# A mixture-of-experts kernel on one core: the place of one row copy in ScalarE's order

## The chip, the cores and the metric

The kernel runs on 1 core of one Trainium2 chip. The metric is the device time of one execution in microseconds (us); lower is better. All times below are in us unless ns stands beside them. The engines are called as in the profile: PE (TensorE), PEld (TensorE's weight loads, which overlap PE), DVE (VectorE), ACT (ScalarE), POOL (GpSimd), SP (SyncE, which here issues DMAs).

## What is computed

A causal convolution over the sequence, with one 7-tap softmax filter for each of 8 heads, gives 28672 rows of 192 numbers. Each row with a positive skip score is then sent to the one of 8 experts whose gate logit is largest, and the expert's two-layer network, scaled by the softmax of that logit, is added to the row:

```python
out = np.einsum('hk,bskhg->bshg', softmax(weight), windows(x))     # (8, 3584, 192)
x = out.reshape(28672, 192)
do_compute = x @ w_skip > 0
xc = x[do_compute]
logits = xc @ w_gate                                               # 8 experts
e_idx = np.argmax(logits, axis=1)
gate_w = softmax(logits)[np.arange(len(xc)), e_idx]
for e in range(8):
    mask = e_idx == e
    h = np.maximum(xc[mask] @ w1[e], 0.0)                          # 192 -> 1024
    y[mask] = gate_w[mask, None] * (h @ w2[e])                     # 1024 -> 192
x[do_compute] = xc + y
```

## The kernel before, in words

The first part (to about 175 us) computes the convolution and the router batch by batch and writes the convolved rows to `out` in device memory. It then makes, for each expert, a list of its rows. The second part goes over these lists in blocks of 256 rows (a few of 128), 61 blocks in all, numbered n: 0 to 7 are from experts 0 and 1 and run while the router finishes; from n = 8 (`NTAIL`) on come 3 more blocks for each of experts 0 and 1 (8 to 13), then 6 for each of experts 2 to 7 (14 to 49; expert e begins at block 14 + 6(e − 2)), then 11 blocks (50 to 60) whose expert is looked up at run time, with weights `wd` that are loaded back from a scratch tensor `wscr`.

All matrix products run in float16, and each number is carried as a high and a low part. For one block there are four steps:

- `gather` (L827): POOL fetches the block's rows by indirect DMA into `y`.
- `prep` (L842): DVE finds a power-of-two scale for each row, ACT writes the scaled high part `yt` (L854), DVE the low part (L859), and SP issues one DMA transpose per 128 rows (L862), which puts the block's columns into `m`, with four slots of 256 rows. Slot 0 holds the high part of the 128 first columns, slot 1 the 64 last columns, high part in partitions 0 to 63 and low part in 64 to 127, slot 2 the low part of the 128 first.
- `up` (L875), the first layer: PE makes 1024 hidden numbers in four PSUM banks `ph`. ACT evicts each bank with a ReLU into `hh` (L908), DVE writes the low part `hl` (L910).
- `down` (L913), the second layer: 24 matmuls of three kinds (L938 to L940) for each 128 rows into `po`; DVE adds the rows (L920), POOL scatters them back (L922).

The step that the change touches lies between `prep` and `up`. The low part of the weights for the 64 last columns is a product with only 64 rows of the array in use. In a block of 256 rows from n = 8 on (`paired`), two such products are put side by side, one in the lower and one in the upper half of the array (L893 to L896). The upper one needs the 64 rows of slot 1 in partitions 64 to 127, so ACT copies them there, into slot 3 (`upper_half`, L838 to L840):

```python
nc.scalar.copy(k.m[64:P, 3, :], k.m[0:64, 1, :])
...
for f, p0, m in ((a + j, 0, 1), (a + fs + j, 64, 3)):
    o = OW1L + F + f * P
    nc.tensor.matmul(phs[f - j][:, j, :], wt[p0:p0 + 64, o:o + P], k.m[p0:p0 + 64, m, 0:w], ...)
```

The copy needs both transposes of its block. Of the eight matmuls (L895) with which such a block opens, the first needs only slot 1, the second needs the copy.

The order on each engine is the order in which the code is written (a manual schedule). The main loop (L1162) writes for each n: the copy of block n+1, `up` of block n+1, `down` of block n. So PE runs up(n+1), down(n), up(n+2), down(n+1) and so on. `weave` (L1143) puts other work between the pieces: after each piece of `up` (four) and `down` (two) `tail_slot` takes one step of background work, then some steps of `prep` follow, which is begun for block n+3 while up(n+1) is written.

The background work is above all `split_weights` (L265), which turns the next expert's float32 weights into high and low parts: seven ACT conversions of 128x512 (L303), each followed a step later by its low part on DVE (L314) and two stores to `wscr` on SP (L318). The first of the seven waits for the scale `ar` (L338, DVE). With six blocks to an expert, the first conversion stands in the second piece of the down in front of the expert's last block; the next three follow the last block's first three evictions of `ph`, and the last three stand between its fourth eviction and the first eviction of the next expert's first block.

Of the kernel before, what the change touches and what calls it, by code (L numbers as in the profile page):

```python
# [16 lines left out]
P = 128  # L17
# [75 lines left out]
def conv_router_moe(ctx: ExitStack, tc: tile.TileContext, x, weight, w_skip, w_gate, w1, w2, out):  # L93
    nc = tc.nc
# [231 lines left out]
    def new_wt(e):  # L326
        if e % 3 == 2:
            return wk3.tile([P, WW], F16, tag="wt", bufs=1, name=f"wt{e}")
        return wst.tile([P, WW], F16, tag="wt", bufs=2, name=f"wt{e}")
# [68 lines left out]
    def store_y(b, half, c0=0, c1=NC):  # L398

        first, n = HALVES[half]  # L400
        t = ys[b, half]
        c0, c1 = max(c0, first), min(c1, first + n)
        full = min(c1, NC - 1)
        for t0, t1 in zip(RSPLIT, RSPLIT[1:]):
            nc.sync.dma_start(out=out[b * S + R * c0:b * S + R * full, :].rearrange("(c t) d -> t c d", t=R)[t0:t1],
                              in_=t[t0:t1, c0 - first:full - first])
        if c1 == NC:
            nc.sync.dma_start(out=out[b * S + R * (NC - 1):(b + 1) * S, :], in_=t[0:LAST, n - 1])
# [426 lines left out]
    def paired(k):  # L835
        return k.us == 2 and NTAIL <= k.n < NBLK

    def upper_half(k):  # L838
        if paired(k):
            nc.scalar.copy(k.m[64:P, 3, :], k.m[0:64, 1, :])  # L840

    def prep(k):  # L842

        am = k.am = wk2.tile([P, 2], F32, tag="yam", bufs=6, name=f"yam{k.n}")
        sc = wk2.tile([P, 2], F32, tag="ysc", bufs=3, name=f"ysc{k.n}")
        nc.vector.tensor_reduce(out=am[:, 0:k.us], in_=k.y[:, 0:k.us], axis=AX.X, op=ALU.max, apply_absolute_value=True)
        yield
        for t, s, op in ((am, am, ALU.bitwise_and), (sc, am, ALU.bitwise_xor)):
            nc.vector.tensor_scalar(out=t[:, 0:k.us].bitcast(I32), in0=s[:, 0:k.us].bitcast(I32), scalar1=EXPMASK,  # L849
                                    scalar2=None, op0=op)  # L850
            yield
        yt = wk2.tile([P, 2, 2 * D], F16, tag="yt", bufs=3, name=f"yt{k.n}")
        for u in range(k.us):
            nc.scalar.activation(yt[:, u, 0:D], k.y[:, u, 0:D], AF.Copy, scale=sc[:, u:u + 1])  # L854
        yield
        k.m = wk2.tile([P, 4, BLK], F16, tag="m", bufs=MBUF, name=f"m{k.n}")
        for u in range(k.us):
            for (a, b_, o) in ((P, D, D), (0, P, D + 64)):
                nc.vector.scalar_tensor_tensor(out=yt[:, u, o:o + b_ - a], in0=k.y[:, u, a:b_],  # L859
                                               scalar=sc[:, u:u + 1], in1=yt[:, u, a:b_],  # L860
                                               op0=ALU.mult, op1=ALU.subtract)
            nc.sync.dma_start_transpose(out=k.m[:, 0:3, u * P:(u + 1) * P], in_=yt[:, u, :])  # L862
            yield

    def finish(gen):
# [5 lines left out]
    def bank(pools):  # L871
        pools.append(pools.pop(0))
        return pools[-1]

    def up(k, wt):  # L875
        k.hh = wk3.tile([P, NF, BLK], F16, tag="hh", bufs=2, name=f"hh{k.n}")
        k.hl = wk3.tile([P, NF, BLK], F16, tag="hl", bufs=2, name=f"hl{k.n}")
        w = k.us * P
        fs = 2 * BLK // w
        seq = ((OW1, 0), (OW1, 2), (OW1 + F, 1), (OW1L, 0), (OW1L + F, 1))  # L880
        phs = {}

        def open_bank(f0):
            phs[f0] = bank(ph_pools).tile([P, 2 * BLK], F32, tag="ph", name=f"ph{k.n}_{f0}").rearrange(
                "p (f w) -> p f w", w=w)

        if paired(k):

            for f0 in range(0, NF, fs):
                open_bank(f0)  # L890
            for a in range(0, NF, 2 * fs):
                for j in range(fs):
                    for f, p0, m in ((a + j, 0, 1), (a + fs + j, 64, 3)):  # L893
                        o = OW1L + F + f * P
                        nc.tensor.matmul(phs[f - j][:, j, :], wt[p0:p0 + 64, o:o + P], k.m[p0:p0 + 64, m, 0:w],  # L895
                                         start=(j == 0), stop=False, tile_position=(p0, 0), skip_group_check=True)  # L896
            seq = seq[:-1]
        for f0 in range(0, NF, fs):
            if not paired(k):
                open_bank(f0)  # L900
            ph = phs[f0]
            for f in range(f0, f0 + fs):
                for n, (o, m) in enumerate(seq):
                    nc.tensor.matmul(ph[:, f - f0, :], wt[:, o + f * P:o + (f + 1) * P], k.m[:, m, 0:w],  # L904
                                     start=(n == 0 and not paired(k)), stop=(n == len(seq) - 1),
                                     skip_group_check=paired(k))
            hh = k.hh[:, f0:f0 + fs, 0:w]
            nc.scalar.activation(hh, ph, AF.Relu)  # L908
            yield
            nc.vector.scalar_tensor_tensor(out=k.hl[:, f0:f0 + fs, 0:w], in0=ph, scalar=0.0, in1=hh,  # L910
                                           op0=ALU.max, op1=ALU.subtract)
# [36 lines left out]
    blocks = []  # L948
# [22 lines left out]
    NBLK = len(blocks)  # L971
# [15 lines left out]
    def weights_of(n):  # L987
        k = blocks[n]
        return wts[k.e] if k.l is None else dynw[k.l]
# [141 lines left out]
    def tail_slot():  # L1131

        background()
        if not listed:
            turns((routes, 0), (routes, 1), (inversions, 0))
            if not routes and not inversions:
                finish(final_lists())
                listed.append(True)
        elif tables:
            if next(tables[0], tables) is tables:  # L1140
                tables.pop()

    def weave(gen, preps=(), n=0):  # L1143

        for _ in gen:
            tail_slot()
            for _ in range(n):
                for p in list(preps):
                    if next(p, p) is p:
                        preps.remove(p)  # L1150
                    else:
                        break
# [9 lines left out]
    for n in range(NBLK):  # L1162
        k = blocks[n]
        if 0 < n < 5:
            store_y(B - 1, n // 3, 8 * n - 8, min(8 * n, NC))
        if n == NTAIL:
            while not past:
                next(tables[0])
            ph1.close()
            wk4 = ctx.enter_context(tc.tile_pool(name="wk4", bufs=1))  # L1170
            ph_pools.append(ctx.enter_context(tc.tile_pool(name="ps_h2", bufs=2, space=PSUM)))
            ph_pools.append(ps_h)
            po_pools.append(ctx.enter_context(tc.tile_pool(name="ps_o2", bufs=2, space=PSUM)))
        nxt = 2 if n == NTAIL - 2 else k.e + 1 if k.e is not None and k.e >= NA and n == first_of[k.e] else E
        if nxt < E:
            wts[nxt] = new_wt(nxt)
            bg.append(split_weights(nxt, wts[nxt]))
        if n + 1 < NBLK and n + 1 == first_of.get(blocks[n + 1].e) and (blocks[n + 1].e or 0) >= NA:
            background(-1)
        m = n + PREP + 1  # L1180
        if m < NBLK and blocks[m].l is not None:
            l = blocks[m].l
            dynw[l] = wk4.tile([P, WW], F16, tag="wd", bufs=5, name=f"wd{l}")
            bg.append(dyn_weights(l, dynw[l]))
        while prepped < min(n + PREP + 1, gathered):
            ahead.append(prep(blocks[prepped]))
            prepped += 1
        if n + 1 < NBLK:
            upper_half(blocks[n + 1])
            weave(up(blocks[n + 1], weights_of(n + 1)), ahead, PU)  # L1190
        ready = NBLK if listed and n > 3 else NTAIL
        if n + 1 >= NTAIL - 2:
            while prepped < min(n + 3, gathered):
                ahead.append(prep(blocks[prepped]))
                prepped += 1
        while gathered < min(n + AHEAD + 1, ready):
            gather(blocks[gathered])
            gathered += 1
        weave(down(k, weights_of(n)), ahead, PD)
        if n + 2 < NBLK and not hasattr(blocks[n + 2], "m"):  # L1200
            if prepped < n + 3:
                ahead.append(prep(blocks[prepped]))
                prepped += 1
            finish(ahead.pop(0))
        if n >= NTAIL + 8 and n % 2 == 0 and (n - NTAIL - 8) // 2 < NDYN:
            dyn_lists((n - NTAIL - 8) // 2)
# [4 lines left out]
    with tc.If(left > 0):  # L1211
# [13 lines left out]
        for e in range(E):  # L1225
            first = nc.values_load(lo_hi[0:1, e:e + 1], min_val=0, max_val=NTOK // BLK)
            last = nc.values_load(lo_hi[0:1, E + e:E + e + 1], min_val=0, max_val=NTOK // BLK)
            with tc.For_i(first, last, 1) as i:
                k = Blk()
# [37 lines left out]
```

## Time and profile before

| what | value |
|---|---|
| time, median of 3 runs | 700.04 (698.31 to 700.28) |
| the profiled execution | 694.53 |
| span in its profile, first to last instruction | 692.8 |
| granted TensorE clock, mean | 0.993 |
| busy: PE, DVE, ACT, POOL | 661.6, 516.5, 338.8, 269.9 |
| start of the first and of the last copy (L840), 48 in all | 259.6, 657.4 |

Rows of the timeline and of the groups read: start and length in us, engine, line of the kernel, operation, output <- input, tile, count, and in brackets how long the engine had stood idle before and what ended that. In the list of waits, a row gives the waiting engine and line, what it waited for, then us in all, times, and the longest. Where the brackets are missing, the engine had no idle time to speak of. Consecutive rows may overlap, since an engine takes the next instruction before the one in front has ended.

### The profile page before, as it was taken

The numbers are of one execution on the slowest core, as the hardware profiler recorded it, in microseconds if no ns is written. First come the engines' busy times: TensorE is split into PE (matmuls) and PEld (weight loads), VectorE is DVE, ScalarE is ACT, GpSimd is POOL, SyncE is SP. The second block draws the span as 40 slices with busy tenths as digits, with TensorE's granted clock in tenths as the row PEclk, the third lists the DMA queues.
The fourth block names the chain that finished last, engine by engine and source line by source line (L and its number), as shares of the span: only waits on it lengthen the run. The fifth ranks groups of instructions, "written<-read, shape, count | busy, mean of one in ns | idle before, by whom it ended". The sixth has DMA issues, their size and how long they took to land. (4 is left out here: it accounts for less than half of the span.)

```text
span 692.8 us, 17693 instructions
## 1 busy us (share of the span) xinstructions
PE 661.6 (96%) x6597; PEld 562.8 (81%) x6597; DVE 516.5 (75%) x1462; ACT 338.8 (49%) x695; POOL 269.9 (39%) x299
## 2 busy tenths in 40 slices
PE   8999899999899999799999999999999999999995
PEld 7667666765689888699888888888888889988995
DVE  7068689878999979678778778778778776666652
ACT  5775486547732333454454554553543644434421
POOL 3111102127013354554644543544444455454322
PEclk9999999999999999999999999999999999999999
DMA  7999999934833455464357365563564446999970
GB/s 211 344 332 323 311 305 330 337 105 99 269 101 95 127 135 112 115 179 133 99 174 155 107 184 130 131 189 105 126 186 118 120 131 162 279 304 286 311 202 15
DMA packets 154403, 129.51 MB, mean 187 GB/s; under 512 B 59600, under 2 KB 141266, under 8 KB 154308
## 3 DMA queue, kind: packets, MB, share of 16 engines
q1 hardware_dynamic: 143268, 106.49, 53.8%
q0 software_dynamic: 11040, 21.80, 12.0%
q8 instruction: 54, 0.88, 0.5%
q14 instruction: 41, 0.34, 0.2%
HBM read 69.70 MB, written 48.04 MB: 170 GB/s over the span
## 5 line engine op out<-in xcount | busy, mean ns | idle before, releaser
L908 ACT ACTIVATE hh<-ph 128x512 f16<-128x512 f32 x230 | 134.5, 594 | 237.6 <-PE ph L904 177.0
L910 DVE SCALAR_TENSOR_TENSOR hl<-ph,hh 128x512 f16<-128x512 f32 x230 | 156.9, 686 | 83.2 <-ACT hh L908 46.1
L940 PE MATMUL po<-wt,hl 128*128 128x192 f16 x768 | 188.9, 246 | 0.9 <-issue 0.9
L938 PE MATMUL po<-wt,hh 128*128 128x192 f16 x768 | 188.9, 246 | 0.9 <-issue 0.7
L939 PE MATMUL po<-wt,hh 128*128 128x192 f16 x768 | 188.9, 246 | 0.5 <-issue 0.4
L904 PE MATMUL ph<-m,wt 128*128 128x256 f16 (+1 forms) x1680 | 186.4, 268 | 2.7 <-DVE yam L849 0.9
L904 PEld LDWEIGHTS <-wt 128*128 128x128 f16 x1680 | 154.2, 98 | 28.8 <-issue 12.4
L922 POOL DMA_INDIRECT out_dram<-o,rows x82 | 84.8, 1035 | 150.5 <-DVE o L920 122.4
L830 POOL DMA_INDIRECT y<-out_dram,rows x82 | 86.1, 1049 | 27.9 <-issue 22.6
L938 PEld LDWEIGHTS <-hh 128*128 128x128 f16 x920 | 90.0, 98 | 2.8 <-issue 2.2
L939 PEld LDWEIGHTS <-hh 128*128 128x128 f16 x920 | 90.0, 98 | 1.8 <-issue 1.2
L940 PEld LDWEIGHTS <-hl 128*128 128x128 f16 x920 | 90.0, 98 | 1.5 <-issue 1.3
L361 PE MATMUL pc<-xs,toep 128*120 128x384 f32 (+1 forms) x224 | 79.8, 480 | 0.0
L920 DVE SCALAR_TENSOR_TENSOR o<-po,yf,y 128x192 f32<-128x192 f32 x115 | 46.6, 414 | 31.4 <-PE po L940 17.2
L363 ACT COPY ys<-pc 120x768 f32<-120x768 f32 (+1 forms) x56 | 42.7, 763 | 43.1 <-PE pc L361 33.4
L859 DVE SCALAR_TENSOR_TENSOR yt<-y,ysc,yt 128x64 f16<-128x64 f32 x230 | 57.8, 311 | 2.6 <-ACT yt L854 2.6
L854 ACT ACTIVATE yt<-y,ysc 128x192 f16<-128x192 f32 x115 | 46.2, 448 | 26.9 <-DVE ysc L849 20.0
L361 PEld LDWEIGHTS pc<-xs,toep 128*120 128x120 f32 x224 | 37.6, 187 | 14.6 <-issue 1.7
L282 DVE TENSOR_REDUCE am<-raw 128x1 f32<-128x512 f32 x56 | 37.9, 676 | 7.8 <-DMA raw<-in_moe_w_dram 7.5
L314 DVE SCALAR_TENSOR_TENSOR wt<-raw,ar,wt 128x512 f16<-128x512 f32 x56 | 41.3, 744 | 1.9 <-ACT wt L303 1.9
L303 ACT ACTIVATE wt<-raw,ar 128x512 f16<-128x512 f32 x56 | 38.8, 727 | 5.1 <-DVE ar L338 5.1
L922 POOL DMA_INDIRECT out_dram<-o,rowsa x14 | 15.5, 1108 | 58.1 <-DVE o L920 49.2
(203 smaller groups left out, 897.8 us busy)
## 6 DMA issues: line engine op xcount, KB each, us to landing
wd<-wscr SPq DMA_DIRECT2D x44, 449.0 KB
wscr<-wt SPq DMA_DIRECT2D x84, 128.0 KB
xs<-in_x_dram SPq DMA_DIRECT2D x7, 1440.0 KB
xs<-in_x_dram SPq DMA_DIRECT2D x7, 1248.0 KB
out_dram<-ys SPq DMA_DIRECT2D x6, 1344.0 KB
out_dram<-ys SPq DMA_DIRECT2D x6, 1092.0 KB
raw<-in_moe_w_dram SPq DMA_DIRECT2D x32, 192.0 KB
raw<-in_moe_w_dram SPq DMA_DIRECT2D x8, 512.0 KB
```

What stands on the lines that cost most here:

```text
L361: nc.tensor.matmul(pc[0:R, i, 0:n * G], toep[:, h + i, :], xs[b, half][:, :, (h + i) * G:(h + i + 1) * G], start=True, stop=True)
L830: rows_apart(nc.gpsimd.indirect_dma_start(out=k.y[:, u, 0:D], out_offset=None, in_=out[0:k.rows, :], in_offset=bass.IndirectOffsetOnAxis(a ...
L854: nc.scalar.activation(yt[:, u, 0:D], k.y[:, u, 0:D], AF.Copy, scale=sc[:, u:u + 1])
L859: nc.vector.scalar_tensor_tensor(out=yt[:, u, o:o + b_ - a], in0=k.y[:, u, a:b_], scalar=sc[:, u:u + 1], in1=yt[:, u, a:b_], op0=ALU.mult, ...
L904: nc.tensor.matmul(ph[:, f - f0, :], wt[:, o + f * P:o + (f + 1) * P], k.m[:, m, 0:w], start=(n == 0 and not paired(k)), stop=(n == len(se ...
L908: nc.scalar.activation(hh, ph, AF.Relu)
L910: nc.vector.scalar_tensor_tensor(out=k.hl[:, f0:f0 + fs, 0:w], in0=ph, scalar=0.0, in1=hh, op0=ALU.max, op1=ALU.subtract)
L920: nc.vector.scalar_tensor_tensor(out=o[:, u, :], in0=po, scalar=f2[:, u:u + 1], in1=k.y[:, u, 0:D], op0=ALU.mult, op1=ALU.add)
L922: rows_apart(nc.gpsimd.indirect_dma_start(out=out[0:k.rows, :], out_offset=bass.IndirectOffsetOnAxis(ap=k.si[:, u, 0:1], axis=0), in_=o[:, ...
L938: nc.tensor.matmul(pos[u], hh, w2(OW2, f), start=(f == 0), stop=False)
L939: nc.tensor.matmul(pos[u], hh, w2(OW2L, f), start=False, stop=False)
L940: nc.tensor.matmul(pos[u], hl, w2(OW2, f), start=False, stop=(f == NF - 1))
```

## The change

`upper_half` is given a block's number instead of the block, remembers which copies are written (`raised`), and asks whether the block's transposes are written already (`turned`, filled by `prep`). The main loop calls it twice: for block n+1 ahead of up(n+1), as before, and for block n+2 directly behind up(n+1), so ahead of down(n). The first call writes nothing if the copy is written already.

```diff
-    def upper_half(k):
-        if paired(k):
-            nc.scalar.copy(k.m[64:P, 3, :], k.m[0:64, 1, :])
+    turned, raised = set(), set()
+
+    def upper_half(n):
+        if n < NBLK and paired(blocks[n]) and n in turned and n not in raised:
+            raised.add(n)
+            nc.scalar.copy(blocks[n].m[64:P, 3, :], blocks[n].m[0:64, 1, :])
...
             nc.sync.dma_start_transpose(out=k.m[:, 0:3, u * P:(u + 1) * P], in_=yt[:, u, :])
+            if u == k.us - 1:
+                turned.add(k.n)
             yield
...
         if n + 1 < NBLK:
-            upper_half(blocks[n + 1])
+            upper_half(n + 1)
             weave(up(blocks[n + 1], weights_of(n + 1)), ahead, PU)
+            upper_half(n + 2)
```

Only ACT's order is changed by it, and there at eleven places. (A name's first number is the block or the expert: `m19` belongs to block 19, `wt3` to expert 3. Line numbers are 3 to 5 higher with the change: L843 is the copy, L913 the eviction.) The first place is block 19, the last block of expert 2, with the last evictions of block 18 ahead of it, on ACT before:

```order
L908 ACTIVATE hh18_5118<-ph18_4_5122 128x512
L908 ACTIVATE hh18_5118<-ph18_6_5123 128x512
L303 ACTIVATE wt3_4675<-raw3_4700,ar3_5019 128x512
L840 COPY m19_5021<-m19_5021 64x256
L908 ACTIVATE hh19_5263<-ph19_0_5265 128x512
```

And the same place on ACT with the change:

```order
L913 ACTIVATE hh18_5118<-ph18_4_5122 128x512
L913 ACTIVATE hh18_5118<-ph18_6_5123 128x512
L843 COPY m19_5021<-m19_5021 64x256
L303 ACTIVATE wt3_4676<-raw3_4700,ar3_5019 128x512
L913 ACTIVATE hh19_5263<-ph19_0_5265 128x512
```

The copy of block 19 has moved ahead of the first conversion of expert 3's weights, the one that waits for the scale. The second place is block 20, the first block of expert 3, on ACT before:

```order
L908 ACTIVATE hh19_5263<-ph19_6_5268 128x512
L303 ACTIVATE wt3_4675<-raw3_4700,ar3_5019 128x512 x3
L840 COPY m20_5172<-m20_5172 64x256
L908 ACTIVATE hh20_5439<-ph20_0_5441 128x512
L908 ACTIVATE hh20_5439<-ph20_2_5442 128x512
```

And the same place on ACT with the change:

```order
L913 ACTIVATE hh19_5263<-ph19_6_5268 128x512
L303 ACTIVATE wt3_4676<-raw3_4700,ar3_5019 128x512
L843 COPY m20_5172<-m20_5172 64x256
L303 ACTIVATE wt3_4676<-raw3_4700,ar3_5019 128x512 x2
L913 ACTIVATE hh20_5439<-ph20_0_5441 128x512
```

The copy of block 20 has moved ahead of the last two of the three conversions; the one that is left ahead of it is written by the background step behind the last piece of `up`. The same two moves stand at the blocks 25 and 26, 31 and 32, 37 and 38, 43 and 44.

The eleventh place is block 13, where expert 2's weights are converted, on ACT before:

```order
L908 ACTIVATE hh12_4262<-ph12_6_4267 128x512
L303 ACTIVATE wt2_3594<-raw2_3619,ar2_4037 128x512 x2
L840 COPY m13_4220<-m13_4220 64x256
L908 ACTIVATE hh13_4386<-ph13_0_4388 128x512
L303 ACTIVATE wt2_3594<-raw2_3619,ar2_4037 128x512
```

And with the change, on ACT at block 13:

```order
L913 ACTIVATE hh12_4262<-ph12_6_4267 128x512
L303 ACTIVATE wt2_3594<-raw2_3619,ar2_4037 128x512
L843 COPY m13_4221<-m13_4221 64x256
L303 ACTIVATE wt2_3594<-raw2_3619,ar2_4037 128x512
L913 ACTIVATE hh13_4386<-ph13_0_4388 128x512
```

Here the copy has passed one conversion of two. At the other 37 copies ACT's rows are the same in both kernels, since no other work for ACT is written between the end of `up` and the next copy.

## The prediction

> **What bounds the kernel now.** I first read the page's busy shares, then the list of who waited for whom, then the lines of the copy, then TensorE's and ACT's timeline at each place where TensorE had waited.
>
> ```profile
> PE 661.6 (96%) x6597; PEld 562.8 (81%) x6597; DVE 516.5 (75%) x1462; ACT 338.8 (49%) x695; POOL 269.9 (39%) x299
> ```
> ```profile
> PE ph L895 <- ACT m L840: 7.2, 8, 2.8
> ...
> PE ph L895 <- ACT wt L303: 0.6, 1, 0.6
> ```
> ```profile
> L840 ACT COPY m<-m x48: 402/403/404, 259.6 to 657.4; 64x256 f16<-64x256 f16 x48
> ```
> ```profile
> L303 ACT ACTIVATE wt<-raw,ar x42: 710/715/729, 287.0 to 553.3; 128x512 f16<-128x512 f32 x42
> ```
>
> TensorE (PE) is the bound, so a stop of PE in the block loop is time. The second view says that of PE's stops the largest item is the wait of the first layer's opening matmuls (L895) for the copy (L840): 7.2 us in 8 waits, and one more wait that is put down to the weight conversion L303, which stands ahead of a copy.
>
> That sum is too small, and the timeline shows why. A block with nothing in its way, from the row of its L895 matmuls to that of L904, and the first block of expert 3 (block 20):
>
> ```profile
> 359.39 0.61 PE L895 MATMUL ph<-m,wt 64*128 64x256 f16 x8
> 359.93 3.67 PE L904 MATMUL ph<-m,wt 128*128 128x256 f16 x32
> ```
> ```profile
> 349.85 0.28 PE L895 MATMUL ph<-m,wt 64*128 64x256 f16 x1
> 351.30 0.59 PE L895 MATMUL ph<-m,wt 64*128 64x256 f16 x7 [1.17 <-ACT m L840]
> 351.83 3.67 PE L904 MATMUL ph<-m,wt 128*128 128x256 f16 x32
> ```
>
> Undisturbed, L904 starts 0.54 after the first L895. At block 20 it is 1.98. The block lost 1.44, not the 1.17 in the bracket, because the first L895 (which reads unshifted rows) is counted busy for 0.28 while its partner stands still. So a place's loss is its bracket plus 0.27; where the eight stand in one row, it is the row's length minus 0.61. The other places:
>
> ```profile
> 292.82 0.59 PE L895 MATMUL ph<-m,wt 64*128 64x256 f16 x7 [2.83 <-ACT m L840]
> ...
> 341.42 0.94 PE L895 MATMUL ph<-m,wt 64*128 64x256 f16 x8
> ...
> 392.91 0.59 PE L895 MATMUL ph<-m,wt 64*128 64x256 f16 x7 [0.23 <-ACT m L840]
> ...
> 401.72 0.59 PE L895 MATMUL ph<-m,wt 64*128 64x256 f16 x7 [0.44 <-ACT m L840]
> ...
> 442.41 0.95 PE L895 MATMUL ph<-m,wt 64*128 64x256 f16 x8
> ...
> 452.45 0.59 PE L895 MATMUL ph<-m,wt 64*128 64x256 f16 x7 [1.32 <-ACT m L840]
> ...
> 494.90 0.59 PE L895 MATMUL ph<-m,wt 64*128 64x256 f16 x7 [0.57 <-ACT wt L303]
> ...
> 503.45 0.59 PE L895 MATMUL ph<-m,wt 64*128 64x256 f16 x7 [0.18 <-ACT m L840]
> ...
> 545.34 0.59 PE L895 MATMUL ph<-m,wt 64*128 64x256 f16 x7 [0.27 <-issue]
> ...
> 554.53 0.59 PE L895 MATMUL ph<-m,wt 64*128 64x256 f16 x7 [0.83 <-ACT m L840]
> ```
>
> The Trainium skill says the same of such rows (Perfetto Trace Analysis, Summary: the profiler window per engine type): a TensorE record ends at an estimated time. Summed by the brackets instead, the gain below would come to about 5.5 us.
>
> **The change part by part.** In the order, 11 of the 48 copies move, and they are those of the eleven places above; each passes one or two L303, and no other engine's order changes, nor any DMA. Nearly all the others stand right behind the evictions already. There are three cases.
>
> *Five blocks that are the last of an expert (19, 25, 31, 37, 43).* The copy stood behind the first L303 of a weight set, which waits for the scale:
>
> ```profile
> 390.15 0.60 ACT L908 ACTIVATE hh<-ph 128x512 f16<-128x512 f32 x1 [0.20 <-remote]
> 391.71 0.72 ACT L303 ACTIVATE wt<-raw,ar 128x512 f16<-128x512 f32 x1 [0.96 <-DVE ar L338]
> 392.46 0.40 ACT L840 COPY m<-m 64x256 f16<-64x256 f16 x1
> ```
>
> Now it goes right behind the eviction, at about 390.8, and ends at 391.2, when PE's first L895 of that block is still 1.2 away (392.91 less 0.23 and 0.28). The L303 waits for the scale as before, so it isn't later. The whole loss goes: 0.33 + 0.50 + 0.34 + 0.84 + 0.54 = 2.55.
>
> *Five blocks that are the first of an expert (20, 26, 32, 38, 44).* Three L303 stood ahead, now one does:
>
> ```profile
> 348.41 0.59 ACT L908 ACTIVATE hh<-ph 128x512 f16<-128x512 f32 x1
> 348.88 1.94 ACT L303 ACTIVATE wt<-raw,ar 128x512 f16<-128x512 f32 x3
> 350.85 0.40 ACT L840 COPY m<-m 64x256 f16<-64x256 f16 x1
> 352.97 0.60 ACT L908 ACTIVATE hh<-ph 128x512 f16<-128x512 f32 x1 [1.72 <-issue]
> ```
>
> Three take 1.94 and one 0.72, so the copy comes 1.22 sooner, at 349.63. Of each loss at most that goes: of 1.44, 0.71, 1.59, 0.45 and 1.10, this is 1.22 + 0.71 + 1.22 + 0.45 + 1.10 = 4.70.
>
> *Block 13.*
>
> ```profile
> 291.01 1.33 ACT L303 ACTIVATE wt<-raw,ar 128x512 f16<-128x512 f32 x2
> 292.37 0.40 ACT L840 COPY m<-m 64x256 f16<-64x256 f16 x1
> ```
>
> One of two L303 is passed: 1.33 − 0.72 = 0.61 of the 3.10 goes. The rest is a late eviction ahead of it, which doesn't move.
>
> Sum: 2.55 + 4.70 + 0.61 = 7.86.
>
> What the move costs: the L303 that are passed come one copy later, 0.40 each. At block 20 the copy would end at 350.03 and the two L303 at 351.38. Three users could feel it. The next eviction on ACT comes 1.67 after PE's second L895 (352.97 − 351.30), so at 351.75 instead of 352.97: 0.37 to spare. DVE's low parts (L314) read those L303:
>
> ```profile
> 351.32 0.74 DVE L314 SCALAR_TENSOR_TENSOR wt<-raw,ar,wt 128x512 f16<-128x512 f32 x1
> ...
> 352.31 0.74 DVE L314 SCALAR_TENSOR_TENSOR wt<-raw,ar,wt 128x512 f16<-128x512 f32 x1
> ...
> 353.63 0.68 DVE L910 SCALAR_TENSOR_TENSOR hl<-ph,hh 128x512 f16<-128x512 f32 x1
> ...
> 355.94 0.68 DVE L910 SCALAR_TENSOR_TENSOR hl<-ph,hh 128x512 f16<-128x512 f32 x1
> ```
> ```profile
> 356.81 0.60 ACT L908 ACTIVATE hh<-ph 128x512 f16<-128x512 f32 x1 [1.11 <-PE ph L904]
> ```
>
> DVE takes them at 351.32 and 352.31, its own order being late already; they would be there at about 350.7 and 351.4. SP's stores of the weight parts follow L314, so they don't move either. I take the cost at nothing; with every margin gone it is 0.40 at six places, 2.4. No gain beside the sum is in sight: ACT is idle half the span.
>
> What is late next: PE comes 1.22 sooner to block 21, at 358.17 instead of 359.39. Its banks need block 20's evictions through DVE. DVE is packed; the third of them (L910) starts at 355.94 as now; the fourth waits for ACT's last eviction, which comes at 355.59 instead of 356.81 and takes 0.60, so it can follow the third directly at 355.94 + 0.68 = 356.62 and end at 357.3. That leaves PE about 0.9.
>
> So the profiled execution, 694.53 with a span of 692.8, would become 686.7. The median of the runs shown, 700.04, is 5.5 longer than it; the order is the same in each, so I take 7.86 off the median: 692.2. Bounds: 5.5 if only the brackets go, 10.9 if all losses went (2.55 + 5.29 + 3.10).
>
> **The rivals.** *The copy waits for its transposes.* It reads what SP's DMA transposes bring, and now comes up to 2 us sooner. For block 20 they are issued here:
>
> ```profile
> 338.72 2.52 SPq L862 DMA_TRANSPOSE m<-yt  x2
> ```
> ```profile
> 267.34 0.40 ACT L840 COPY m<-m 64x256 f16<-64x256 f16 x1 [0.55 <-DMA m<-yt]
> ```
>
> The row is of the issue. The Trainium skill (Perfetto Trace Analysis, DMA Instruction — HWDGE) says that such a row leaves out the data's movement, which speaks against the change: the rows may not be there at 341.24. If they land only when the copies run now, every copy waits, ACT's L303 behind it too, and nothing is gained: 700.0. Against it: 8.4 us lie between issue and the new place (349.63), and of the 48 copies just one waited for a transpose, 0.55, though most of the 37 that stay put already stand right behind the evictions, where the eleven come to stand. 7%.
>
> *DVE becomes the bound where experts change.* The window of block 44 and one without conversions (window, its length, then busy us of PE, PEld, DVE, ACT, POOL, clock, DMA):
>
> ```profile
> 550.00:560.00 10.00, 9.17 (x101) 8.24 (x99) 9.40 (x24) 6.77 (x13) 4.37 (x4) 1.00 0.68 209
> ```
> ```profile
> 560.00:600.00 40.00, 40.00 (x437) 36.24 (x435) 24.47 (x65) 15.99 (x33) 20.54 (x20) 1.00 0.67 170
> ```
>
> DVE has 9.40 of 10 there. If the margin of 0.9 at block 21 is not real, PE stops at the banks instead of at the copy, and the 4.70 of the second case is given back: 2.55 + 0.61 stay, 696.9. Against it: after it DVE has 24.47 of 40, so it catches up. 13%, of which 5% within 0.3% of before.
>
> *PE's clock falls when its gaps close*, which would make the kernel slower. It acts from block 13 on to the last block, about 390 us; each per cent of clock costs 3.9. From 2.0% the gain is gone, and at 2.8% it is 10.9 − 7.9 = 3.0 slower: 703. Against it: in the 40 us where PE has no gap, the clock is 1.00. 4%.
>
> *The change doesn't do what it says* in one respect: "sooner" holds for eleven copies only, and the sum counts only these. Something that doesn't move with PE could also eat the gain at the end, the dynamic weights above all:
>
> ```profile
> 578.92 1.44 SPq L984 DMA_DIRECT2D wd<-wscr  x3
> ```
> ```profile
> L895 PEld LDWEIGHTS <-wd x64: 92/94/96, 603.1 to 660.8; 64*128 64x128 f16 x64
> ```
>
> They are issued between transposes that follow the blocks, 24 us ahead of use, so they move along; I give it no chance of its own.
>
> **How the numbers follow.** The forecast has 76%: 692.2. DVE 13%, transposes 7%, clock 4%. Low end: 692.2 less the 1.7 by which the lowest run shown (698.31) lies under its median, 690.5. High end: the DVE case, 696.9, which takes in the 5.5 of the brackets (694.5) and the 2.4 of cost. This leaves out transposes, clock and the strays. About 0.3% (2.1 us) is what a measurement of this kernel can tell from no change. Faster: 76 + 8 = 84%; same: 5 + 7 = 12%; slower: 4%.
>
> **What would show it.** Right: the wait of L895 for the copy falls from 7.2 to about 2.9 (block 13's 2.2, and the rests of blocks 20 and 32), the five last blocks show eight L895 in 0.61, and from block 44 on everything stands about 7.9 sooner. Wrong: copies with idle time ended by a DMA (transposes), L895 or L904 ended by the low part L910 (DVE), a clock under 0.98 in the windows, or a tail that starts sooner and ends when it did.

## The result and the profile after

The changed kernel takes 694.68 us (median of 14 runs, 688.38 to 699.29), the kernel before, measured beside it, 700.6 (14 runs, 698.28 to 705.89). The ratio is 0.9891 [0.9859, 0.9923], which is 7.6 us less [5.4, 9.9]. (The ratio, here and below, is taken over the runs and not over the two medians, which lie 5.9 apart.) The forecast was 7.86 less, 692.2, in a range from 690.5 to 696.9.

The profiled execution of the changed kernel is the longest of its runs, a disturbed one (699.29, span 697.5, clock 0.986). Its single places can be read; its span is not set beside that of before.

The waits of PE in the changed kernel (engine, operation, line, what it waited for: us in all, times, longest):

```profile
PE ph L900 <- ACT m L843: 2.1, 2, 2.0
...
PE ph L909 <- DVE hl L915: 0.7, 1, 0.7
```

The wait for the copy has gone from 7.2 us in 8 waits to 2.1 in 2. The wait for DVE's low part (L915) is what it was before, 0.7 in one. PE's opening matmuls at the five last blocks of an expert (19, 25, 31, 37, 43), in the same kernel:

```profile
346.00 0.61 PE L900 MATMUL ph<-m,wt 64*128 64x256 f16 x8
...
396.88 0.61 PE L900 MATMUL ph<-m,wt 64*128 64x256 f16 x8
...
447.52 0.61 PE L900 MATMUL ph<-m,wt 64*128 64x256 f16 x8
...
498.89 0.61 PE L900 MATMUL ph<-m,wt 64*128 64x256 f16 x8
...
549.25 0.61 PE L900 MATMUL ph<-m,wt 64*128 64x256 f16 x8
```

All five are whole: eight matmuls in 0.61. The first blocks (20, 26, 32, 38, 44), and ahead of them block 13:

```profile
295.17 0.77 PE L900 MATMUL ph<-m,wt 64*128 64x256 f16 x7 [1.97 <-ACT m L843]
...
354.33 0.65 PE L900 MATMUL ph<-m,wt 64*128 64x256 f16 x8
...
405.19 1.01 PE L900 MATMUL ph<-m,wt 64*128 64x256 f16 x8
...
455.63 1.00 PE L900 MATMUL ph<-m,wt 64*128 64x256 f16 x8
...
507.72 0.59 PE L900 MATMUL ph<-m,wt 64*128 64x256 f16 x7 [0.15 <-ACT m L843]
...
557.57 0.81 PE L900 MATMUL ph<-m,wt 64*128 64x256 f16 x8
```

By the prediction's rule (row less 0.61, or bracket plus 0.27) the first blocks keep 0.04, 0.40, 0.40, 0.42 and 0.20, together 1.46. Block 13 keeps 2.24 by the rule and 2.41 from start to end, since its row of seven is 0.18 longer than the 0.59 of the others. The eleven places lost 10.94 before and lose 3.87 now: 7.1 less. ACT at block 20 shows the move itself:

```profile
353.19 0.72 ACT L303 ACTIVATE wt<-raw,ar 128x512 f16<-128x512 f32 x1
353.94 0.40 ACT L843 COPY m<-m 64x256 f16<-64x256 f16 x1
354.37 1.33 ACT L303 ACTIVATE wt<-raw,ar 128x512 f16<-128x512 f32 x2
356.06 0.60 ACT L913 ACTIVATE hh<-ph 128x512 f16<-128x512 f32 x1 [0.36 <-PE ph L909]
```

One conversion stands ahead of the copy, two behind it, and the next eviction still waits for PE, so the passed conversions delay nothing there. The clock (the column after POOL's) in the stretch of the ten blocks:

```profile
345.00:560.00 215.00, 210.12 (x2237) 186.21 (x2236) 169.81 (x448) 108.15 (x211) 107.08 (x105) 1.00 0.55 144
```

PE's clock does not fall where its gaps close. Yet this execution gained nothing in the blocks from 19 to 57. Their last opening matmuls in it, and then in the profile before:

```profile
665.43 0.61 PE L900 MATMUL ph<-m,wd 64*128 64x256 f16 x8
```

(changed kernel, begun at 346.00), and

```profile
660.57 0.61 PE L895 MATMUL ph<-m,wd 64*128 64x256 f16 x8
```

(kernel before, begun at 341.42). That is 319.43 against 319.15. What the places gave, this long execution lost again behind the opening matmuls. Block by block (from start to start, less 8.10), the 28 blocks that are neither first nor last of an expert went from 3.3 to 6.9. The ten others went only from 8.1 to 4.7, though their openings gave 6.3. In the second layer PE's waits that end on nothing the profile names ("issue") are 5.8 in 17 over the whole run, against 2.2 in 8 before. Whether that belongs to the change had to be seen in executions that lie nearer to their medians (set 2).

### The profile page after: what moved, and what is told of

It reads as the page before. It is cut to its first block, busy times and chain, and to the rows that moved or that the text cites. A ratio compares the mean times of both kernels' runs of the same rounds, so it can differ in the third digit from the quotient of the medians.

```text
span 697.5 us, 17693 instructions
## 1 busy us (share of the span) xinstructions
PE 667.6 (96%) x6597; PEld 564.4 (81%) x6597; DVE 514.4 (74%) x1462; ACT 340.3 (49%) x695; POOL 268.3 (38%) x299
## 4 chain that ended last, share of the span: by engine, by line
PE 59%; DVE 2%; issue 2%; ACT 2%; DMA 0%; another core or an unknown queue 0%; POOL 0%; POOLq 0%
PE ph L909 27%; PE po L944 10%; PE po L945 9%; PE po L943 9%; PE ph L900 4%; ACT wt L303 1%; DVE hl L915 1%; DVE o L925 0%; DMA m<-yt 0%; ACT hh L913 0%; ACT m L843 0%; ACT yt L857 0%; DVE yt L862 0%; DVE yam L849 0%
## 5 line engine op out<-in xcount | busy, mean ns | idle before, releaser
L913 ACT ACTIVATE hh<-ph 128x512 f16<-128x512 f32 x230 | 133.9, 594 | 239.2 <-PE ph L909 173.9
L915 DVE SCALAR_TENSOR_TENSOR hl<-ph,hh 128x512 f16<-128x512 f32 x230 | 156.3, 687 | 91.7 <-ACT hh L913 61.7
L909 PE MATMUL ph<-m,wt 128*128 128x256 f16 (+1 forms) x1680 | 189.7, 270 | 3.0 <-issue 0.9
```

## The experiments

They ran in four sets; the kernels of a set share the runs of the kernel before. Two theories stood at the outset. **Copy:** the time comes from the places, about 2.5 at last blocks, 4.7 at first blocks and 0.6 at block 13. **Given back:** closing a place moves the stop to a later one, so that the parts don't add up to the whole.

### Set 1: the whole, its two parts, and a doubled cost

*again* is the changed kernel. *last_only* moves the copy at last blocks alone, *first_only* at block 13 and the first blocks alone:

```diff
             weave(up(blocks[n + 1], weights_of(n + 1)), ahead, PU)
-            upper_half(n + 2)
+            if n + 2 in (19, 25, 31, 37, 43):               # last_only
+            if n + 2 in (13, 20, 26, 32, 38, 44):           # first_only
+                upper_half(n + 2)
```

*dose* is the kernel before with two ACT operations of 128x512 more (0.627 each, from a constant into a tile that nobody reads) ahead of the copy at the ten last and first blocks; nothing of the computation is left out:

```diff
         if paired(k):
+            if k.n in (19, 20, 25, 26, 31, 32, 37, 38, 43, 44):
+                for _ in range(2):
+                    junk = wk3.tile([P, 512], F16, tag="junk", bufs=1, name=f"junk{k.n}_{_}")
+                    nc.scalar.activation(junk.rearrange("p (a b) -> p a b", b=P), ones16.unsqueeze(1).broadcast_to([P, 4, P]), AF.Copy)
             nc.scalar.copy(k.m[64:P, 3, :], k.m[0:64, 1, :])
```

> The changed kernel unaltered. Theory A (PE stood still at eleven places until a copy came, and a place's loss is read from the starts of L895 and L904): 7.9 us less than before, about 692; the wait of the opening matmuls for the copy about 2.3 us at block 13 and 0.2 to 0.4 at blocks 20 and 32, none elsewhere. Theory B (only the idle time in the brackets was lost): 5.5 us less, about 694.5. Rival C (DVE is the bound where experts change): about 3 us less, and PE waits for L910 at blocks 21, 27, 33, 39, 45.

> Only the copies of the five last blocks of an expert (19, 25, 31, 37, 43) move, past one conversion that waits for the scale. Theory A: 2.5 us less than before; these five blocks open with eight L895 in 0.61, and the first blocks (20, 26, 32, 38, 44) lose as much as before, about 1.4, 0.7, 1.6, 0.4, 1.1. Theory B: 1.1 less. Rival C': what a last block gains, its expert's next block waits longer, since ACT's conversions and not PE set that copy: nothing less, and the five first blocks lose 0.3 to 0.8 more.

> Only the copies of block 13 and of the five first blocks (20, 26, 32, 38, 44) move, past one or two conversions. Theory A: 4.7 + 0.6 = 5.3 us less than before; the five last blocks lose what they lost before, 0.3 to 0.8 each. Theory B: 4.5 less. Rival C (DVE gives it back): about 0.6 less, with waits for L910 two block steps later.

> The kernel before, with two more ACT operations of 128x512 (a copy of a constant into a tile nobody reads, about 0.6 us each) ahead of the copy at the ten places where experts change. Theory A: every one of the ten places already waits for its copy, so each loses some 1.2 us more: about 12 us more than before, 712, and the brackets of L895 at the ten places grow by 1.2. Rival C (DVE or another engine sets the pace there, the copy's wait is only what shows): under 5 us more.

Measured, the kernel before at 676.85 (28 runs):

| kernel | us | ratio to before | us against before |
|---|---|---|---|
| again | 673.66 | 0.9955 [0.9937, 0.9973] | 3.1 less [1.8, 4.3] |
| last_only | 676.77 | 1.0004 [0.9986, 1.0022] | none |
| first_only | 673.66 | 0.997 [0.9954, 0.9985] | 2.0 less [1.0, 3.1] |
| dose | 684.9 | 1.0132 [1.0102, 1.0161] | 8.9 more [6.9, 10.9] |

The kernel before is itself 24 us shorter here than in the first measurement, the change brings less than half of the forecast, and its first part nothing. (Below, these times about 677 are called the regular level, those of the first measurement the higher one.) The 7.9, 2.5 and 5.3 that theory *Copy* had put on the three kernels all failed on this level. In *last_only* the first blocks are as before the change; blocks 19 to 21 on PE there:

```profile
335.63 0.61 PE L900 MATMUL ph<-m,wt 64*128 64x256 f16 x8
...
343.73 0.28 PE L900 MATMUL ph<-m,wt 64*128 64x256 f16 x1
...
344.19 0.59 PE L900 MATMUL ph<-m,wt 64*128 64x256 f16 x7 [0.18 <-ACT m L843]
...
352.28 0.61 PE L900 MATMUL ph<-m,wt 64*128 64x256 f16 x8
```

From block 19 to 20 it takes 8.10, from 20 to 21 8.55. The bracket is 0.18 and the block loses 0.45: the 0.27 that the prediction added is real. But 0.45 is far from the 1.44 of the first profile. The five first blocks of *last_only* are alike, so with the 0.6 of block 13 there are 5 × 0.45 + 0.6 = 2.9 us to be had in all, which agrees with *again* and with *first_only*. The last blocks have nothing to give: in *first_only*, where their copies stand as before the change, all five are whole. Block 19 there:

```profile
332.71 0.61 PE L900 MATMUL ph<-m,wt 64*128 64x256 f16 x8
```

The parts add up to the whole, so nothing here speaks for *given back*. Blocks 19, 21 and 57 in *again*:

```profile
333.98 0.61 PE L900 MATMUL ph<-m,wt 64*128 64x256 f16 x8
...
350.19 0.61 PE L900 MATMUL ph<-m,wt 64*128 64x256 f16 x8
...
641.90 0.61 PE L900 MATMUL ph<-m,wd 64*128 64x256 f16 x8
```

From block 19 to 21 it takes 16.21. From block 19 to block 57, 38 blocks, it takes 307.92, which is 38 times 8.10: not one stop is left there.

Why were the losses larger in the first profile? The conversions take the same time (0.73 each in the mean in both); what differs is when ACT's evictions come. Block 21 shows it, whose first-layer matmuls run at the regular pace in both: in the kernel before they are the rows at 359.39 and 359.93 that the prediction shows. ACT's first two evictions of that block, in the kernel before:

```profile
362.15 0.60 ACT L908 ACTIVATE hh<-ph 128x512 f16<-128x512 f32 x1 [4.31 <-PE ph L904]
364.96 0.60 ACT L908 ACTIVATE hh<-ph 128x512 f16<-128x512 f32 x1 [2.21 <-PE ph L904]
```

And in *again*, where the block begins at 350.19, PE's main matmuls and the same two evictions:

```profile
350.73 3.67 PE L909 MATMUL ph<-m,wt 128*128 128x256 f16 x32
...
351.88 0.60 ACT L913 ACTIVATE hh<-ph 128x512 f16<-128x512 f32 x1 [3.77 <-PE ph L909]
352.69 0.60 ACT L913 ACTIVATE hh<-ph 128x512 f16<-128x512 f32 x1 [0.21 <-PE ph L909]
```

PE's rows are alike, yet the evictions come 2.76 and 5.57 after the block's start in one and 1.69 and 2.50 in the other. What comes later in ACT's order in front of a copy can make the copy as much later. What ACT's evictions wait for between 300 and 660, first in the kernel before as first profiled:

```profile
ACT hh L908 <- PE ph L904: 132.1, 92, 4.3
ACT hh L908 <- issue: 31.3, 18, 3.6
ACT hh L908 <- remote: 6.7, 11, 1.5
```

And in *again*, the only row of them:

```profile
ACT hh L913 <- PE ph L909: 172.3, 87, 4.5
```

These sums don't show the lateness: they come to 170.1 and 172.3, nearly the same. What shows it is how far behind the matmul that ends its bank each eviction begins, read instruction by instruction over the blocks 19 to 56, wherever ACT stood idle in front of it. In *again* and in *first_only* that is 0.31 to 0.37 after the matmul's start at all 72 places. In the first profile it is over 0.45 at 64 of 110 places, in the middle 1.6 and at most 3.4; a recorded signal of PE's stands within 0.15 of each of the 64 evictions. So ACT is not late by its own order: PE's signal comes late, behind matmuls that start on time. ("issue" is mostly not lateness: 17 of those 18 begin 0.31 to 0.37 behind their matmul.)

*dose* tests the cause directly. At a last block and the first block behind it, and at the next block:

```profile
333.41 0.59 PE L899 MATMUL ph<-m,wt 64*128 64x256 f16 x7 [0.31 <-ACT m L844]
...
341.50 0.28 PE L899 MATMUL ph<-m,wt 64*128 64x256 f16 x1
...
343.07 0.59 PE L899 MATMUL ph<-m,wt 64*128 64x256 f16 x7 [1.30 <-ACT m L844]
...
351.16 0.61 PE L899 MATMUL ph<-m,wt 64*128 64x256 f16 x8
```

The first block's bracket has grown from 0.18 to 1.30, and its period is 9.66. So the two operations, which overlap a little, delay the copy by 1.12. The last block, which had slack, loses the part of this that the slack didn't hold, 0.58. Five of each: 5 × 1.12 + 5 × (0.31 + 0.27) = 8.5, measured 8.9. The expectation took all ten at their full price, which is where it was too high. The price is the excess of ACT's work ahead of the copy over the slack.

### Set 2: the same, and the copy still sooner

*before_here* is the kernel before, unaltered, profiled once more, and *again_2* the changed kernel. *right_behind* and *early* move the copy on from there, into `up`, behind the last eviction of the block in front, or behind its second:

```diff
             nc.scalar.activation(hh, ph, AF.Relu)
+            if f0 + fs >= NF:               # right_behind
+            if f0 >= 2:                     # early
+                upper_half(k.n + 1)
             yield
```

> The kernel before, unaltered, for a trace beside the ones of this chip. Theory A' (PE waits at the first blocks in any case, at the last blocks only where ACT's evictions come late by themselves): if the evictions come 1.7 us after a block's first L895 throughout, brackets of 0.18 at the five first blocks, 1.27 at block 13 and none at the last blocks; if many come 2 us and more after it, larger brackets at both, up to those of the trace shown at the start. Rival (the waits of that trace belong to that kernel and that order): the same brackets as there on every chip.

> The changed kernel unaltered, a second time. Theory A': 2.9 us less than before where the evictions are regular, up to 7.9 where they are not. Rival: 7.9 less everywhere, and the 3.1 measured before was chance.

> The copy stands directly behind the last eviction of the block in front, ahead of the one conversion that is still ahead of it with the change, at block 13 and the five first blocks. Theory A': block 13's bracket falls by the conversion's 0.6, and no first block has one: 0.6 less than the changed kernel where the evictions are regular, about 1.2 less where they are not. Rival (a conversion that comes later holds DVE and the banks): the same as the changed kernel or slower, with waits for L910's evictions through DVE.

> The copy stands behind the second of the four evictions of the block in front, about 2.5 us sooner still. Theory A': no opening wait for the copy anywhere except by the transposes; block 13's remaining wait goes too, about 0.9 less than the changed kernel where the evictions are regular, up to 3 where they are not. Rival C'' (the transposes have not landed by then): ACT stands idle in front of copies until a DMA ends, evictions come later, and the kernel is slower than the changed one by the sum of these waits, 0.3 to 1 each at 48 copies at worst.

Measured, the kernel before at 693.91 (20 runs): *before_here* 691.33 in its one run; *again_2* 686.4, 0.9903 [0.9869, 0.9936], 6.7 less [4.4, 9.1]; *right_behind* 685.9, 0.9896 [0.986, 0.9932], the same as the change; *early* 690.16, 0.9968 [0.9936, 0.9999], 2.2 less, so worse than the change by some 4.

This set is like the first measurement, in its level and in its gain. The waits of *before_here* on PE:

```profile
PE ph L895 <- ACT m L840: 6.5, 8, 2.9
```

They stand at nearly the places and have nearly the sizes of the first profile: by the prediction's rules the change should take 4.04 at first blocks, 2.42 at last blocks and 0.61 at block 13 from this one, 7.07; it took 6.7. The two profiles of this set can be set beside each other. Blocks 19 and 57 in *before_here*:

```profile
338.79 0.85 PE L895 MATMUL ph<-m,wt 64*128 64x256 f16 x8
...
657.10 0.61 PE L895 MATMUL ph<-m,wd 64*128 64x256 f16 x8
```

And in *again_2*:

```profile
341.42 0.61 PE L900 MATMUL ph<-m,wt 64*128 64x256 f16 x8
...
654.20 0.61 PE L900 MATMUL ph<-m,wd 64*128 64x256 f16 x8
```

The 38 blocks take 318.31 and 312.78, against 307.92 in set 1. So 10.4 over the regular pace has become 4.9. Taken block by block (from start to start, less 8.10), the ten first and last blocks have gone from 7.8 to 2.7, the other 28 from 2.7 to 2.3. So in this pair the change does not lengthen the other blocks, and what they lost in the first profile after belongs to that execution.

*right_behind* takes away what the change leaves at the first blocks: *again_2* still waits there for the copy (brackets of 0.23 and 0.25 at blocks 20 and 26), *right_behind* nowhere. By the rows the first blocks keep 1.38 in one and 0.59 in the other. The expectation was 1.2 less than the change; measured is 0.5, which the noise doesn't tell from nothing. It was also expected to take 0.6 from block 13. Block 13 in *again_2*:

```profile
291.75 0.59 PE L900 MATMUL ph<-m,wt 64*128 64x256 f16 x7 [1.59 <-ACT m L843]
```

And in *right_behind*:

```profile
288.26 0.70 PE L900 MATMUL ph<-m,wt 64*128 64x256 f16 x7 [1.66 <-ACT m L843]
```

The bracket stays, though the last conversion is out of the way. ACT's last eviction of block 12 and the copy of block 13, in *again_2*:

```profile
290.07 0.60 ACT L913 ACTIVATE hh<-ph 128x512 f16<-128x512 f32 x1 [0.33 <-PE po L945]
...
291.30 0.40 ACT L843 COPY m<-m 64x256 f16<-64x256 f16 x1
```

And in *right_behind*:

```profile
287.20 0.59 ACT L913 ACTIVATE hh<-ph 128x512 f16<-128x512 f32 x1
287.81 0.40 ACT L843 COPY m<-m 64x256 f16<-64x256 f16 x1
```

The copy starts 1.23 behind the eviction in the first and 0.61 in the second, so the conversion's 0.6 is gone. But the eviction begins 0.18 after the block's first matmul (289.89) in the first and 0.88 after it (286.32) in the second: in that execution it was 0.7 later, which hid the gain. So much of the rest at block 13 is an eviction's lateness, and it differs from one execution to the next.

*early* shows what lies beyond. Its ACT at a copy:

```profile
263.24 0.40 ACT L843 COPY m<-m 64x256 f16<-64x256 f16 x1 [2.67 <-DMA m<-yt]
```

And PE behind it:

```profile
265.38 0.40 PE L900 MATMUL ph<-m,wt 64*128 64x256 f16 x4 [1.31 <-DVE hl L917]
```

The copy now waits for its transposes, as five of the 48 copies do there (6.1 in all, where *again_2* has one of 0.7), and the evictions that stand behind it on ACT wait with it; DVE's low part needs them, and PE its bank. PE's waits in *early*:

```profile
PE ph L900 <- DVE hl L917: 3.9, 6, 1.3
...
PE ph L900 <- DMA m<-yt: 0.9, 1, 0.9
PE ph L900 <- DVE wt L314: 0.8, 2, 0.5
```

That is 5.6 in all, where *again_2* has 3.4 (2.6 for the copy, 0.8 for a DMA). These 2.2 are some half of what *early* is worse by in its medians; the rest was not found. The two profiled executions themselves differ by only 1.0 (689.02 and 688.01), so they can't settle it.

### Set 3: the two parts again

> Only the copies of the five last blocks of an expert move, a second time, in case this chip brings ACT's evictions late as the ones of the first profile and of the second set did. Theory A': if the evictions are regular, the same as before; if not, about 2.4 us less (0.24 + 0.70 + 0.82 + 0.66 by the trace of before in the second set), and the first blocks lose what they lost before. Rival C' (the gain of a last block is given back at the next block's copy, which ACT's conversions set): nothing less either way, and the first blocks lose 0.3 to 0.8 more.

> Only the copies of block 13 and of the five first blocks move, a second time. Theory A': if the evictions are regular, 2.9 us less than before; if not, about 4.7 less (4.0 + 0.6 by the trace of before in the second set), so more than the last blocks alone. Rival C (DVE gives it back): under 1 less, with waits for the evictions through DVE.

Measured, the kernel before at 677.08 (23 runs): *last_only_2* 676.6, 0.9989 [0.9972, 1.0005]; *first_only_2* 673.86, 0.9959 [0.9942, 0.9976], 2.8 less [1.6, 3.9]. This set fell on the regular level again, and agrees with set 1. So the question for which it was made, whether the last blocks' 2.5 is given back where there is something to gain at them, was not answered by the parts.

### Set 4: evictions made late

If late evictions make the copy's place matter, making them late on the regular level must make the change worth more there. *late_before* is the kernel before, *late_after* the changed one, each with two more ACT operations (as in *dose*) ahead of the second eviction of ten blocks, which are those in front of the last and the first ones; nothing is left out:

```diff
             hh = k.hh[:, f0:f0 + fs, 0:w]
+            if f0 == 2 and k.n in (18, 19, 24, 25, 30, 31, 36, 37, 42, 43):
+                for i in range(2):
+                    junk = wk3.tile([P, 512], F16, tag="junk", bufs=1, name=f"junk{k.n}_{i}")
+                    nc.scalar.activation(junk.rearrange("p (a b) -> p a b", b=P),
+                                         ones16.unsqueeze(1).broadcast_to([P, 4, P]), AF.Copy)
             nc.scalar.activation(hh, ph, AF.Relu)
```

> The kernel before, with ACT's evictions made late: two ACT operations that nobody reads (0.63 us each, about 1.1 together) ahead of the second eviction of the last two blocks of experts 2 to 6 (blocks 18 and 19, 24 and 25, and so on), the blocks in front of the copies that the change moves. Theory A' (the loss at a copy grows with how late ACT is): on a chip with regular evictions the five first blocks lose 1.1 more each (brackets from 0.18 to about 1.2) and the five last ones 0.2 to 0.5, together 6 to 8 more than before, 682 to 685 where before has 677. Rival (lateness on ACT isn't what sets these waits): under 2 more.

> The changed kernel with the same late evictions at the same places. Theory A': the moved copies take most of the lateness up, brackets at the first blocks at most about 0.2 and none at the last: near the changed kernel without them, so 1 to 3 less than before, and 6 to 9 less than the other kernel of this pair, in place of the 3 that the change brought with regular evictions. Rival: as much over the changed kernel as the other of the pair lies over the kernel before, so the same difference of about 3.

Measured, the kernel before at 676.44 (17 runs): *late_before* 683.79, 1.0101 [1.0083, 1.0118], 6.8 more [5.6, 8.0]; *late_after* 676.06, 0.9986 [0.9972, 1.0], 0.9 less. The change is now worth 7.7, where it is worth 3.1 in set 1. A last and a first block in *late_before*:

```profile
333.94 0.86 PE L895 MATMUL ph<-m,wt 64*128 64x256 f16 x8
...
343.88 0.59 PE L895 MATMUL ph<-m,wt 64*128 64x256 f16 x7 [1.30 <-ACT m L840]
```

And the first block in *late_after*:

```profile
343.51 1.00 PE L900 MATMUL ph<-m,wt 64*128 64x256 f16 x8
```

In *late_before* five last blocks lose 0.25 and five first blocks 1.57, 9.1 in all, where 2.25 was lost without the delay: 6.85 more, measured 6.8. In *late_after* the last blocks show 0.61, and the first ones keep 0.39 each, 1.95; it takes 2.4 more than *again*, across two sets. By the places the pair should differ by 9.1 − 1.95 + 0.6 (block 13) = 7.75. The delay alone brings the forecast's size onto the regular level, and at last blocks too the gain is there as soon as the evictions are late (1.25 of it). The delay here is ACT's own work, though; that PE's late signals do the same on the higher level is argued from the traces, not produced by a run.

## Why the prediction was right, and where its sum was not safe

- **The bound.** The opening matmuls waited for the copy, and time followed from it: *dose* adds it, the change takes it, and in sets 1, 2 and 4 both go by the places' sums.
- **Bracket plus 0.27.** Shown by the period: 8.55 against 8.10 with a bracket of 0.18. The alternative, brackets alone, falls on that. By time alone *dose* could not have told it (5 × 1.12 + 5 × 0.31 = 7.15 lies in its interval too).
- **Last blocks, 2.55.** All five are whole in the profile after. Where the last blocks had nothing to lose (sets 1 and 3), moving them brought nothing. On a level where they lose of themselves, that part was never run alone; *late_after* shows it with added delays only.
- **First blocks, 4.70.** The rests are 1.46 where 0.59 was forecast, so 3.8 by the rows. The term was 0.9 too high: the last eviction in front of the copy comes 6.7 to 7.2 after its block's start at all five, where it is 5.7 in *again*, and the copy can't pass it.
- **Block 13, 0.61 of 3.10.** 0.69 by the rows (3.10 to 2.41). Of what stays, 0.92 stays in *again* too; the other 1.5 goes with the late evictions of the higher level.
- **The conversions passed at no cost.** No wait of PE for them or for DVE's low part is new in the profile after; in *again* the blocks from 19 to 57 have no stop, which leaves no room for a cost there.
- **The step that failed: "the order is the same in each, so I take 7.86 off the median."** The order is the same, but the losses are not made by the order alone. They come from the order and the lateness of ACT's evictions together, and the lateness differs: 7.6 and 6.7 where the kernel before takes 700.6 and 693.91; 3.1 where it takes 676.85. The forecast held by luck in this one respect: the measurement fell on the level of the profile. That the terms were 0.9 too high at first blocks and 0.1 too low at block 13 did not show either. The gain is not a property of the two programs alone.
- **Its signs of being right.** The wait for the copy fell to 2.1 (2.9 forecast), and the five last blocks are whole. The third sign, everything 7.9 sooner from block 44 on, is not in the profile after, which is the longest execution and begins block 19 already 4.6 later.
- **The rivals.** Transposes: wrong for this change (two waits of the copy for a DMA, 0.9 in all, in the profile after), but right for five copies of *early*, with waits of up to 2.67. DVE: not the bound here; in *early* its low part becomes what PE waits for, at 265.38 because ACT's copy stands in front of the eviction that it needs (the other five of these waits were not followed up). Clock: 1.00 where the gaps closed. Tail: in set 2 the blocks gain 5.5, and the total 6.7.

## What to carry to other kernels

A small operation that gates the bound engine should stand, in the order of a shared engine, behind what it needs and ahead of what nobody waits for; the best place is a window, and half a block further its own inputs were not there at five of 48 places. Price such a move by the period from block to block, not by the bracket of the wait. And before a loss read from one execution is taken for the kernel's, look at whether the loop is regular in it: whether each consumer that stood idle begins equally far behind what it waits for. Here it did where the change brought 3.1, and did not where it brought 6.7 and 7.6. The name that a list of waits gives to idle time does not tell this.

## What the runs showed of the hardware

The same unaltered program took about 677 in three sets and 694 to 701 in the two other measurements. Sets 1 and 2, one on each level, are recorded under the same chip number (3) and a quarter of an hour apart, so the number alone does not decide the level; for the first measurement no number is recorded.

On the regular level the 38 blocks of *again* and of *first_only* take 8.10 each, and every eviction that ACT stood idle for begins 0.31 to 0.37 after the start of the matmul that ends its bank. The kernel before has no profile of its own there. On the higher one 64 to 73 of such evictions come later in each of four profiles (before and after, *before_here*, *again_2*), up to 3.7 behind that matmul. The stretch of 38 blocks is 10.4 longer in *before_here* than in *again*, of which the change took 5.5.

What is late is PE's signal to ACT, and not every signal: DVE's low part, where DVE stood idle for it, begins 0.03 behind the end of its eviction on both levels (66 places in the first profile, 29 in *again*), and the second opening matmul 0.05 behind its copy. The profile records when a matmul starts and models its end, so whether PE ends late or only its signal is late can't be read from it.

The losses of two profiles of the kernel before on the higher level stand at nearly the same blocks, so they are not noise of one execution; the clock is 0.993 and 0.998 there and 0.992 in *again*, so it is not the clock. What makes PE's signals late is open.
